# GpSimd's instructions in program order, the first expert's W2 squares in a chain of their own, and two experts' W1 products in halves of the tokens

## The chip, the cores and the metric

The kernel runs on one core of a Trainium2 chip. The metric is the device time of one execution in microseconds (us), the median of several runs. Five engines run their own instruction streams and wait for each other by semaphores: TensorE (PE in the profile), VectorE (DVE), ScalarE (ACT), GpSimd (POOL) and SyncE (SP, which only issues transfers here). Transfers are also issued by GpSimd, where rows are gathered or scattered by a list of row numbers.

## The reference, cut to what matters

First an attention over 8 batches and 8 heads of 576 positions (half of the heads with a band of 32 positions, half with every 32nd position), and then a layer of 8 experts on its output. The change is in the second part:

```python
def _moe_ref(x, w_gate, w1, w2):              # x: 4608 x 512, from the attention
    N, D = x.shape
    E = w_gate.shape[1]                        # 8
    cap = N // E                               # 576
    logits = x @ w_gate
    flat = logits.flatten()
    order = np.argsort(-flat)
    assigned = -np.ones(N, dtype=np.int64)
    counts = np.zeros(E, dtype=np.int64)
    for idx in order:
        tok, e = (int(idx) // E, int(idx) % E)
        if assigned[tok] >= 0 or counts[e] >= cap:
            continue
        assigned[tok] = e
        counts[e] += 1
        if (assigned >= 0).all():
            break
    out = np.zeros((N, D), dtype=np.float32)
    for e in range(E):
        mask = assigned == e
        h = np.maximum(x[mask] @ w1[e], 0.0)   # 576 x 1024
        out[mask] = h @ w2[e]                  # 576 x 512
    return out.astype(np.float32)
```

Each expert takes exactly 576 tokens, and which ones it takes depends on the experts that were filled before it.

## The kernel before, in words

Until about 262 us of the profiled execution the core does the attention, writes its rows to a scratch tensor in DRAM (`x_scr`) and finds the first expert's tokens. From then on it works through the experts, in the order in which they fill up, as phases 0 to 7; "expert 1" below is the expert of phase 1. A phase has these steps.

- **Search.** Some rounds narrow down the threshold at which the expert is full: VectorE compares (`cm`, L848), TensorE sums (L867, L876, L886), VectorE takes the next step (L871, L874, L884).
- **Indices.** The tokens above the threshold are numbered (L912 to L949), one-hot tiles are made (`ohl`, L992), 36 small TensorE products (L1001) and two more (L1012) turn them into a list of 576 row numbers, `idx` (L1016, L1017). Search and indices of a later expert run between the products of an earlier one.
- **Tokens.** `tokens()` has GpSimd gather the rows in five blocks of 128, 128, 128, 128 and 64 tokens (`xg`, L1168, from `x_scr`), and SyncE's queue transpose each block into `xt` (L1171). Blocks 0 to 2 of expert 0 are transposed by TensorE (L1154).
- **Weights.** W1 and W2 come in four loads of 512 KB each (`w`, L1041, SyncE's queue). ScalarE sums their squares (`jk`, L1045), from which a power of two is derived as a scale (L1051, L1056, L207). Then ScalarE makes the high halves (`w1h`, `w2h`, L1062) and VectorE the low ones (`w1l`, `w2l`, L1066), in float16, eight pieces of each matrix.
- **W1 products.** `hidden()` makes one of eight tiles of 128 hidden units for a list of column ranges (12 products a range, L1260); ScalarE takes the high half of the result (`hh`, L1266), VectorE the low half (`hl`, L1270). Expert 0 goes through all eight tiles for tokens 0 to 255 and then through all eight for tokens 256 to 575. The others do both 288-token halves of a tile before the next tile.
- **W2 products.** In `ffn()` token blocks 0 and 1 go first, as a pair (48 products, L1324), then the 64 tokens of block 4 as the tail (24 half-width products, L1312), then blocks 2 and 3 (24 products each, L1324). Within the pair the pieces of W2 are used in order, with the products `w2h·hh`, `w2l·hh`, `w2h·hl` for each block. ScalarE writes the result `y` (L1337; the tail's by ScalarE and VectorE, L1332 and L1333), and GpSimd scatters its rows to the output (L1338): five scatters per expert, which touch different rows.

The order of all this on TensorE, ScalarE, VectorE and SyncE is the order in which the program emits it (`manual_schedule`, with the engine sets `MAN` and `MAN1`, L49). GpSimd's order before is made by the compiler's own scheduler. The program's order comes from a planner that runs at build time: each side task (search of the next expert, fetch, splits, the low half of a tile) is a Python generator in the list `chains` with a due time. The loop at the end walks through the TensorE products, adds their assumed cost to `clock`, and advances every chain whose due time has come. `busy` holds the assumed end of what is queued on ScalarE and VectorE, `book()` adds to it, and `idle()` waits until it is short. The numbers `T_...` are due times in ns: `fetch()` of an expert yields `T_LOAD`, the time it allows from the request of the tokens until the expert may start, `T_W20` is the due time of expert 0's W2 squares, and the clock runs at double cost until `T_COLD`. The due times only set an order. Nothing on the chip waits for a clock.

All scatters write the same DRAM tensor, so that by the framework's rule a later one would wait for an earlier one. The kernel before takes this off by name:

```python
            for s in scat:
                tc.declare_no_dep(st.ins, s.ins, reason="rows of other tokens")
            scat.append(st)
```

## Time and profile before

| what | value |
|---|---|
| runs shown | 704.23, 706.38, 708.78 us (median 706.38) |
| profiled execution | 700.24 us, of which its span is 698.4 us |
| TensorE busy | 607.0 us (87%) |
| VectorE, ScalarE, GpSimd busy | 460.5, 320.0, 152.9 us |
| TensorE busy, 386 to 690 us | 299.78 of 304.00 us |
| TensorE busy, 296 to 304, 319 to 330, 376 to 386 us | 5.28 of 8.00, 6.17 of 11.00, 7.82 of 10.00 us |

The page of the profile gives busy times by engine, the same in 40 slices with the clock that TensorE was granted (PEclk), and the costliest groups of instructions with what ended the idle time before them. Other views answer for a stretch of time: what TensorE waited for, the single instructions in order, and the transfers with the time from issue to landing. Busy times of TensorE overlap from one instruction to the next, so that the distance between starts is what a product costs.

### The profile page before, as it was taken

The numbers are of one execution on the slowest core, as the hardware profiler recorded it, in microseconds if no ns is written. First come the engines' busy times: TensorE is split into PE (matmuls) and PEld (weight loads), VectorE is DVE, ScalarE is ACT, GpSimd is POOL, SyncE is SP. The second block draws the span as 40 slices with busy tenths as digits, with TensorE's granted clock in tenths as the row PEclk, the third lists the DMA queues.
The fourth block names the chain that finished last, engine by engine and source line by source line (L and its number), as shares of the span: only waits on it lengthen the run. The fifth ranks groups of instructions, "written<-read, shape, count | busy, mean of one in ns | idle before, by whom it ended". The sixth has DMA issues, their size and how long they took to land.

```text
span 698.4 us, 19162 instructions
## 1 busy us (share of the span) xinstructions
PE 607.0 (87%) x8044; PEld 400.2 (57%) x8044; DVE 460.5 (66%) x1371; ACT 320.0 (46%) x499; POOL 152.9 (22%) x151
## 2 busy tenths in 40 slices
PE   6768689887886449987998999999999999999993
PEld 3556466665665428544853864764764765755741
DVE  4588476776887778854886788886786864561200
ACT  3455336345443046433565465645545576572210
POOL 2044133233143020032032032023202122202011
PEclk9587767888899569998999999999999999999997
DMA  9989999899765064239167275368366296731010
GB/s 248 267 210 235 235 255 219 217 263 236 182 141 130 2 218 115 70 116 260 45 175 211 67 197 183 137 106 253 120 105 207 107 217 233 205 44 69 1 39 30
DMA packets 107081, 111.23 MB, mean 159 GB/s; under 512 B 75852, under 2 KB 83622, under 8 KB 106483
## 3 DMA queue, kind: packets, MB, share of 16 engines
q1 hardware_dynamic: 98915, 88.46, 49.4%
q0 software_dynamic: 7360, 21.15, 9.8%
q8 instruction: 63, 1.03, 0.6%
q10 hardware_dynamic: 720, 0.39, 0.2%
q14 instruction: 23, 0.19, 0.1%
HBM read 73.60 MB, written 18.87 MB: 132 GB/s over the span
## 4 chain that ended last, share of the span: by engine, by line
PE 36%; issue 17%; DVE 3%; POOL 2%; DMA 1%; SPq 0%; ACT 0%; POOLq 0%; ACTq 0%
PE ph L1260 17%; PE ph L1324 14%; PE ph L1312 2%; POOL out_dram L1338 1%; POOL xg L1168 1%; DMA w<-in_w_dram 1%; DMA xg<-x_scr,idx 1%; DVE w2l L1066 0%; SPq L1171 0%; PE ph L1154 0%; DVE hl L1270 0%; DVE ohl L992 0%; ACT w1h L1062 0%; PE ph L1201 0%; PE pr__8414 L1001 0%
## 5 line engine op out<-in xcount | busy, mean ns | idle before, releaser
L1260 PE MATMUL ph<-xt,w1h 128*128 128x288 f16 (+2 forms) x1024 | 174.7, 287 | 5.4 <-DMA xt<-xg 4.8
L1260 PEld LDWEIGHTS <-w1h 128*128 128x128 f16 x1024 | 97.5, 98 | 31.3 <-issue 3.7
L1260 PE MATMUL ph<-xt,w1l 128*128 128x288 f16 (+2 forms) x512 | 110.8, 287 | 0.0
L1324 PE MATMUL ph<-w2l,hh 128*128 128x512 f16 x256 | 98.3, 384 | 4.8 <-DVE w2l L1066 4.7
L1324 PE MATMUL ph<-w2h,hl 128*128 128x512 f16 x256 | 98.4, 384 | 0.0
L1324 PE MATMUL ph<-w2h,hh 128*128 128x512 f16 x256 | 97.9, 383 | 0.0
L1338 POOL DMA_INDIRECT out_dram<-y,idx x40 | 42.6, 1066 | 235.9 <-ACT y L1337 222.0
L1266 ACT ACTIVATE hh<-ph 128x576 f16<-128x576 f32 (+2 forms) x72 | 42.9, 596 | 99.7 <-PE ph L1260 94.3
L1045 ACT ACTIVATE jk<-w 128x1024 f16<-128x1024 f32 x64 | 67.3, 1052 | 41.5 <-DMA w<-in_w_dram 40.6
L1324 PEld LDWEIGHTS <-hh 128*128 128x128 f16 x512 | 48.6, 98 | 59.3 <-issue 8.6
L1168 POOL DMA_INDIRECT xg<-x_scr,idx x40 | 41.1, 1028 | 145.4 <-DVE idx L1016 65.0
L1270 DVE SCALAR_TENSOR_TENSOR hl<-ph,hh 128x576 f16<-128x576 f32 (+2 forms) x72 | 49.2, 684 | 30.7 <-ACT hh L1266 30.5
L379 ACT ACTIVATE pr<-spa 128x576 f32<-128x576 f32 x32 | 20.8, 650 | 97.5 <-PE spa L375 97.5
L1260 PEld LDWEIGHTS <-w1l 128*128 128x128 f16 x512 | 49.6, 98 | 12.6 <-issue 0.4
L1337 ACT ACTIVATE y<-ph,so 128x512 f32<-128x512 f32 x32 | 21.1, 684 | 75.2 <-PE ph L1324 73.3
L427 POOL TENSOR_TENSOR xos<-xs,xos 118x768 f16<-118x768 f32 x16 | 27.4, 1712 | 121.9 <-ACT xos L426 121.9
L396 PE MATMUL po<-v_s,pr 64*54 64x65 f32 (+1 forms) x768 | 42.8, 264 | 10.7 <-issue 6.4
L1066 DVE SCALAR_TENSOR_TENSOR w2l<-w,w_sw,w2h 128x512 f16<-128x512 f32 x64 | 46.2, 744 | 4.2 <-ACT w2h L1062 4.2
L1066 DVE SCALAR_TENSOR_TENSOR w1l<-w,w_sw,w1h 128x512 f16<-128x512 f32 x64 | 46.4, 744 | 3.8 <-ACT w1h L1062 3.7
L1062 ACT ACTIVATE w2h<-w,w_sw 128x512 f16<-128x512 f32 x64 | 42.7, 712 | 12.2 <-DVE w_sw L207 12.2
L1062 ACT ACTIVATE w1h<-w,w_sw 128x512 f16<-128x512 f32 x64 | 42.2, 712 | 9.5 <-DVE w_sw L207 8.2
L1324 PEld LDWEIGHTS <-hl 128*128 128x128 f16 x256 | 25.1, 98 | 32.8 <-issue 7.5
(616 smaller groups left out, 952.4 us busy)
## 6 DMA issues: line engine op xcount, KB each, us to landing
w<-in_w_dram SPq DMA_DIRECT2D x64, 512.0 KB
kl<-in_kl_dram SPq DMA_DIRECT2D x8, 608.0 KB
v_s<-in_ns_dram SPq DMA_DIRECT2D x16, 292.5 KB
v_l<-in_nl_dram SPq DMA_DIRECT2D x16, 292.5 KB
ql<-in_qt_dram SPq DMA_DIRECT2D x8, 576.0 KB
x_scr<-xol SPq DMA_DIRECT2D x8, 512.0 KB
ks<-in_ks_dram SPq DMA_DIRECT2D x7, 576.0 KB
qs<-in_qt_dram SPq DMA_DIRECT2D x7, 576.0 KB
```

The lines of the kernel that those rows point to most:

```text
L396: nc.tensor.matmul(po[r:r + n, j - j0], pr[k, o:o + n], u.vn[k, t, 2 * p + h], start=(j == j0), stop=(j == j1 - 1), skip_group_check=True)
L427: eng.tensor_tensor(u.xo[:nr, :, 1, c], xf, u.xo[:nr, :, 0, c], op=OP.subtract)
L1045: nc.scalar.activation(jk, wf[:, c * n4:(c + 1) * n4].rearrange("p c f -> p (c f)"), AF.Square, scale=1.41422, accum_out=sq[:, c:c + 1])
L1062: nc.scalar.activation(hi[:, c, f], wf[:, c, f], AF.Copy, scale=s_)
L1066: nc.vector.scalar_tensor_tensor(lo[:, c, f], wf[:, c, f], s_, hi[:, c, f], op0=OP.mult, op1=OP.subtract)
L1168: nc.gpsimd.indirect_dma_start(out=xg[:n], out_offset=None, in_=x_rows, in_offset=bass.IndirectOffsetOnAxis(ap=idx[:n, t:t + 1], axis=0))
L1260: nc.tensor.matmul(tile_[:, j, :w], wt[:, d, f * 128:(f + 1) * 128], xt[:, d // 2, xx, d % 2, c], start=(k == 0), stop=(k == 3 * DC - 1))
L1266: nc.scalar.activation(hv, src, AF.Relu)
L1270: nc.vector.scalar_tensor_tensor(lv, src, 0.0, hv, op0=OP.max, op1=OP.subtract)
L1324: nc.tensor.matmul(pair[:, u], a[:, f, (t + u) * 128:(t + u) * 128 + 128], w[:, f], start=(f == 0 and a is hh and w is w2h), stop=(f == FC ...
L1337: nc.scalar.activation(y, py, AF.Copy, scale=so[:, t:t + 1])
L1338: st = nc.gpsimd.indirect_dma_start(out=out_rows, out_offset=bass.IndirectOffsetOnAxis(ap=idx[:n, t:t + 1], axis=0), in_=y[:n], in_offset= ...
```

## The change

Five things are altered. GpSimd joins the engines whose instructions stand in program order. The squares and the scale of expert 0's W2 (`sums()`) become a chain that the planner may advance by itself; the chain that splits W1 and W2 still runs through it, and each of the four squares has a due time of its own instead of one for all. The first two experts (`HALVES`) make their W1 products in two ranges, tokens 0 to 255 and 256 to 575, in this order: tiles 0 to 3 for the first range, tiles 4 to 7 for both, tiles 0 to 3 for the second; their `fetch()` yields 8500 instead of 12000. `T_COLD` becomes 1500. And the list `scat` with its `declare_no_dep` is gone.

```diff
-MAN, MAN1 = {mybir.EngineType.PE}, {mybir.EngineType.Activation, mybir.EngineType.DVE, mybir.EngineType.SP}
+MAN, MAN1 = {mybir.EngineType.PE}, {mybir.EngineType.Activation, mybir.EngineType.DVE, mybir.EngineType.SP,
+                                       mybir.EngineType.Pool}
...
-T_LOAD, T_LOAD0, T_W20, T_LAND1, T_LAND2, T_TURN, T_COLD, CUT0, T_ROUND0 = 12000, 1500, 9000, 9000, 8500, 11000, 5000, 1, 1600
+HALVES, T_HALF, T_LOAD, T_LOAD0, T_W20, T_LAND1, T_LAND2, T_TURN, T_COLD, CUT0, T_ROUND0 = 2, 8500, 12000, 1500, (5000, 9500, 11500, 13000), 9000, 8500, 11000, 1500, 1, 1600
...
             def squares(land):
-                yield due(land)
                 for c in range(4):
+                    yield due(land if isinstance(land, int) else land[c])
                     yield from idle("s", 0)
                     square(c)
...
+            def sums():
+                yield from squares2(T_W20)
+                yield from scale2()
+
+            sums_ = sums()
+
             def later():
                 yield from splits1(CUT0)
-                yield from squares2(T_W20)
-                yield from scale2()
+                yield from sums_
                 yield from splits2()
...
                 chains.append([clock, bulk[-1]])
+                chains.append([clock, sums_])
...
-        yield T_LOAD
+        yield T_HALF if ph < HALVES else T_LOAD
...
-        if ph == 0:
+        if ph < HALVES:
             t0 = H0 // 128
-            for f in first[TURN_E:t0]:
-                f()
-            for c in (slice(0, H0), slice(H0, CAP)):
-                for f in range(FC):
-                    yield from hidden(ph, wts, xt, hh, hl, f, (c,), ps_h.tile([128, 2, 512], F32, name="ph"))
-                    if c.start == 0 and max(t0, TURN_E) <= t0 + f < len(first):
-                        first[t0 + f]()
+            part = slice(0, H0), slice(H0, CAP)
+            for u, f in [(0, f) for f in range(FC // 2)] + [(u, f) for f in range(FC // 2, FC) for u in range(2)] + \
+                    [(1, f) for f in range(FC // 2)]:
+                yield from hidden(ph, wts, xt, hh, hl, f, (part[u],), ps_h.tile([128, 2, 512], F32, name="ph"))
+                if ph == 0 and u == 0 and max(t0, TURN_E) <= t0 + f < len(first):
+                    first[t0 + f]()
...
-                        for c in (0, H0 if ph == 0 else 0):
+                        for c in (0, H0 if ph < HALVES else 0):
...
-                st = nc.gpsimd.indirect_dma_start(out=out_rows,
-                                                  out_offset=bass.IndirectOffsetOnAxis(ap=idx[:n, t:t + 1], axis=0),
-                                                  in_=y[:n], in_offset=None)
-            for s in scat:
-                tc.declare_no_dep(st.ins, s.ins, reason="rows of other tokens")
-            scat.append(st)
+                nc.gpsimd.indirect_dma_start(out=out_rows,
+                                             out_offset=bass.IndirectOffsetOnAxis(ap=idx[:n, t:t + 1], axis=0),
+                                             in_=y[:n], in_offset=None)
```

In the changed kernel L1168 becomes L1175, L1338 becomes L1344, L1066 becomes L1067, L1012 becomes L1013, L1312 becomes L1318 and L1324 becomes L1330.

On GpSimd, from the first scatter of expert 0 on, the kernel before has these instructions. `out_dram<-y,idx` is a scatter, `xg<-x_scr,idx` a gather, `DMASW` with a number is the landing of an earlier transfer that GpSimd issued, `Activation` and `DVE` are the engines that write `y` or `idx`, `DMAHW` is the landing of a transfer of SyncE's queue.

```order
L1338 DMA out_dram<-y,idx 4608x512 [waits Activation_49] x2
L1168 DMA xg<-x_scr,idx 128x1024 [waits DMASW7_49,DVE_49]
L1168 DMA xg<-x_scr,idx 128x1024 [waits DMASW0_49,PE_49]
L1168 DMA xg<-x_scr,idx 128x1024 [waits DMAHW5_49,DMASW2_49]
L1168 DMA xg<-x_scr,idx 128x1024 [waits DMAHW6_49,DMASW3_49,DMASW1_49]
L1168 DMA xg<-x_scr,idx 64x1024 [waits PE_49]
L1338 DMA out_dram<-y,idx 4608x512 [waits DVE_49]
L1338 DMA out_dram<-y,idx 4608x512 [waits DMASW4_49,Activation_49]
L1338 DMA out_dram<-y,idx 4608x512 [waits DMASW5_49,Activation_49]
L1168 DMA xg<-x_scr,idx 128x1024 [waits DMAHW6_49,DMASW6_49,DVE_49]
```

The changed kernel has at the same place:

```order
L1344 DMA out_dram<-y,idx 4608x512 [waits Activation_49]
L1344 DMA out_dram<-y,idx 4608x512 [waits DMASW4_49,Activation_49]
L1344 DMA out_dram<-y,idx 4608x512 [waits DMASW5_49,DVE_49]
L1175 DMA xg<-x_scr,idx 128x1024 [waits DMASW7_49,DVE_49]
L1175 DMA xg<-x_scr,idx 128x1024 [waits DMASW0_49,PE_49]
L1175 DMA xg<-x_scr,idx 64x1024 [waits PE_49]
L1344 DMA out_dram<-y,idx 4608x512 [waits DMASW6_49,Activation_49]
L1344 DMA out_dram<-y,idx 4608x512 [waits DMASW4_49,Activation_49]
L1344 DMA out_dram<-y,idx 4608x512 [waits DMASW5_49,Activation_49]
L1344 DMA out_dram<-y,idx 4608x512 [waits DMASW7_49,DMASW6_49,Activation_49]
L1175 DMA xg<-x_scr,idx 128x1024 [waits DMAHW6_49,DMASW0_49,DVE_49]
```

(Two of expert 1's five gathers are left out of this piece.) Two scatters of expert 0 stood ahead of expert 1's gathers, and now three do. The gathers of expert 2 stood ahead of all scatters of expert 1, and now stand behind the first two of them. Each scatter but the first now waits for the landing of the scatter ahead of it: the `DMASW4` of the second is the landing of the first, the `DMASW5` of the third that of the second, and so on. In the kernel before, the `DMASW` of a scatter is a transfer eight issues back.

On VectorE, at the end of expert 0's W2 splits, with expert 1's indices between them, the kernel before has (`sc`, `slot`, `ohh`, `rv` and `ohl` belong to the indices; rows left out stand between these):

```order
L1066 SCALAR_TENSOR_TENSOR w2l<-w_4037,w_sw_4039,w2h 128x512
L943 TENSOR_SCALAR off<-sc 128x72
L949 TENSOR_TENSOR slot<-off 128x36
L1066 SCALAR_TENSOR_TENSOR w2l<-w_4037,w_sw_4039,w2h 128x512
L974 CAST si<-slot 128x36
L984 TENSOR_TENSOR rv_3688<-ohh,val 128x972
L992 TENSOR_TENSOR ohl_4772<-sh,iota 128x768
L961 TENSOR_TENSOR L<-L,pe_4751 128x288
L1066 SCALAR_TENSOR_TENSOR w2l<-w_4037,w_sw_4039,w2h 128x512 x3
```

And the changed kernel:

```order
L932 TENSOR_TENSOR sc<-sc 128x36
L1067 SCALAR_TENSOR_TENSOR w2l<-w_4037,w_sw_4039,w2h 128x512 x2
L944 TENSOR_SCALAR off<-sc 128x72
L950 TENSOR_TENSOR slot<-off 128x36
L975 CAST si<-slot 128x36
L985 TENSOR_TENSOR rv_3688<-ohh,val 128x972
L993 TENSOR_TENSOR ohl_4789<-sh,iota 128x768
L1067 SCALAR_TENSOR_TENSOR w2l<-w_4037,w_sw_4039,w2h 128x512
L962 TENSOR_TENSOR L<-L,pe_4770 128x288
```

Three of the eight low halves stood behind the indices, and now one does, the eighth.

On TensorE, the last two index products of expert 1 (`pick`, L1012) stood between the tail products of expert 0:

```order
L1312 MATMUL ph<-w2h,hh 64x512
L1012 LDWEIGHTS p_4843
L1012 MATMUL pr__4868<-pick,p_4843 64x10
L1312 LDWEIGHTS hh
L1312 MATMUL ph<-w2l,hh 64x512
```

In the changed kernel they stand behind all 24 of them:

```order
L1318 MATMUL ph<-w2h,hl 64x512
L1330 LDWEIGHTS hh
L1330 MATMUL ph<-w2h,hh 128x512
L1013 LDWEIGHTS p_4871
L1013 MATMUL pr__4891<-pick,p_4871 64x10
L1330 LDWEIGHTS hh
```

They moved by 17 products: 16 of the tail and one of block 2. The 36 products L1001 that feed them moved from inside the pair into the tail.

More of the change, by code (lines that the diff above doesn't have):

```diff
@@ L743, in band_stride_attention_then_capacity_moe @@
     x_rows = x_scr.rearrange("n a d -> n (a d)")
-    scat, closed, first = [], [], []
+    closed, first = [], []
     ready, emitted = set(), set()
```

## The prediction

> **What bounds the kernel now.** I read the page first: which engine is busy, and when.
>
> ```profile
> span 698.4 us, 19162 instructions
> PE 607.0 (87%) x8044; PEld 400.2 (57%) x8044; DVE 460.5 (66%) x1371; ACT 320.0 (46%) x499; POOL 152.9 (22%) x151
> PE   6768689887886449987998999999999999999993
> ```
>
> TensorE carries the span. The experts begin at the 16th slice (17.5 us each), and from the 21st on its digit is 9. The change touches nothing ahead of the experts, so the question is which microseconds TensorE loses behind 262 us. Its busy time by stretches, and what it waited for from 255 us on, say where they lie:
>
> ```profile
> 296.00:304.00 8.00, 5.28 (x40) 2.29 (x42) 4.36 (x9) 0.96 (x2) 0.00 (x0) 0.79 0.37 149
> 319.00:330.00 11.00, 6.17 (x37) 3.75 (x35) 3.15 (x10) 0.69 (x1) 1.00 (x1) 0.69 1.06 282
> 376.00:386.00 10.00, 7.82 (x53) 4.04 (x52) 4.72 (x14) 3.98 (x7) 1.88 (x2) 0.83 0.29 110
> 386.00:690.00 304.00, 299.78 (x2325) 188.48 (x2323) 185.22 (x546) 151.46 (x250) 57.30 (x56) 1.00 0.47 133
> ...
> PE ph L1260 <- DMA xt<-xg: 4.8, 2, 2.9
> PE ph L1324 <- DVE w2l L1066: 4.7, 5, 2.8
> ...
> PE pr__5819 L876 <- DVE r L874: 2.2, 1, 2.2
> ```
>
> (The first number behind the stretch is TensorE's busy time; the last three are its granted clock, the DMA share and GB/s.) From 386 us on it is 99% busy at clock 1.00. The losses lie in three places: A (296 to 304, W2's low halves of expert 0), B (319 to 330, expert 1's tokens) and C (376 to 386, a search step). The single instructions give their prices:
>
> ```profile
> 298.72 0.58 PE L1324 MATMUL ph<-w2l,hh 128*128 128x512 f16 x1 [2.80 <-DVE w2l L1066]
> 302.07 0.38 PE L1324 MATMUL ph<-w2h,hh 128*128 128x512 f16 x1
> 302.28 0.38 PE L1324 MATMUL ph<-w2l,hh 128*128 128x512 f16 x1
> ...
> 305.44 1.05 PE L1312 MATMUL ph<-w2h,hh 128*64 128x512 f16 x8
> ...
> 319.76 0.17 PE L886 MATMUL pr__5037<-ih,ones_j 128*128 128x1 f16 x1
> 322.84 0.40 PE L1260 MATMUL ph<-xt,w1h 128*128 128x288 f16 x1 [2.91 <-DMA xt<-xg]
> 325.16 0.90 PE L1260 MATMUL ph<-xt,w1h 128*128 128x288 f16 x3 [1.92 <-DMA xt<-xg]
> 328.80 0.64 PE L1260 MATMUL ph<-xt,w1h 128*128 128x288 f16 x2
> ...
> 365.36 1.05 PE L1312 MATMUL ph<-w2h,hh 128*64 128x512 f16 x8
> ...
> 380.49 0.17 PE L876 MATMUL pr__5819<-r,fold 68*128 68x8 f16 x1 [2.19 <-DVE r L874]
> 383.90 0.69 PE L1260 MATMUL ph<-xt,w1h 128*128 128x288 f16 x4
> ```
>
> At full clock a W2 product costs 302.28 - 302.07 = 0.21 us. In A the 8 products from 298.72 to 302.07 took 3.35 instead of 1.7 us, so that a wait of 2.80 us brought 1.6 us of half speed after it: A = 4.4. In B the waits are 2.91 and 1.92, the one product between them cost 0.3 too much, and from 325.16 to 328.80 some 1.75 of 3.64 us are half speed: B = 6.9. In C, 2.19 plus about 1.6: C = 3.8. Two later waits for `w2l` in expert 1 make 0.7. Together 15.8 us are lost here, and everything that the change moves lies here.
>
> [...] In A, after 2.80 us of idleness, products ran at half speed. [...]
>
> **The change, part by part.** *Scatters that wait for each other.* The removed `declare_no_dep` and the order rows say that each scatter now waits on GpSimd for the previous one's landing, with the gathers queued behind it. GpSimd in the trace:
>
> ```profile
> 306.52 1.03 POOL L1338 DMA_INDIRECT out_dram<-y,idx  x1 [46.52 <-ACT y L1337]
> 307.85 0.98 POOL L1338 DMA_INDIRECT out_dram<-y,idx  x1 [0.30 <-ACT jk L1045]
> 309.14 1.15 POOL L1168 DMA_INDIRECT xg<-x_scr,idx  x1 [0.30 <-DVE cm L848]
> ...
> 356.87 0.99 POOL L1168 DMA_INDIRECT xg<-x_scr,idx  x1 [34.95 <-DVE idx L1016]
> ...
> 367.48 1.04 POOL L1338 DMA_INDIRECT out_dram<-y,idx  x1 [3.22 <-ACT y L1337]
> 368.83 1.21 POOL L1338 DMA_INDIRECT out_dram<-y,idx  x1 [0.30 <-issue]
> ...
> 682.95 0.98 POOL L1338 DMA_INDIRECT out_dram<-y,idx  x1 [3.65 <-ACT y L1337]
> 688.12 0.97 POOL L1338 DMA_INDIRECT out_dram<-y,idx  x1 [4.20 <-ACT y L1337]
> ```
>
> and the landings, from issue, of the two scatters issued at 306.52 and 307.85, of the one at 367.48, of the one at 370.76 (under weight loads), and of all ten in 296 to 395 us:
>
> ```profile
> out_dram<-y,idx POOLq DMA_INDIRECT x2, 2.8
> ...
> out_dram<-y,idx POOLq DMA_INDIRECT x1, 3.0
> ...
> out_dram<-y,idx POOLq DMA_INDIRECT x1, 6.5
> ...
> out_dram<-y,idx POOLq DMA_INDIRECT x10, 3.4
> ```
>
> So one wait costs 2.8 to 6.5 us where 1.3 us of issue stood; I take 2.8 next to expert 0 and 3.0 next to expert 1. Let P be the start of the tail (305.44, 365.36). Expert 0: scatters at P + 1.1, P + 4.0 and P + 6.9, first gather 1.3 later at X = P + 8.2; it was P + 3.7. Expert 1: first scatter P + 2.1, second P + 5.1, gathers of expert 2 at X = P + 6.4 (5.2 at the least, 9.9 with a landing of 6.5); they were 8.5 us ahead of P.
>
> [...]
>
> *Halves (B).* From X, expert 1's third block was in place at 322.84 (X + 13.7) and the fifth at 325.16 (X + 16.0). Both halves were needed at once; the first range now needs two blocks. One block less is 1.15 us by these two, so X + 12.5. A block's issue is 1.2 to 3.2 us long:
>
> ```profile
> L1171 SPq DMA_TRANSPOSE xt<-xg x37: 1192/1452/3178, 261.5 to 613.8; - x37
> ```
>
> which bounds it to X + 10.5. So products start at P + 20.7 (18.7 at the least). TensorE gets there at P + 15.3: 319.93 - 305.44 = 14.5, plus the 36 products L1001 that now stand behind the pair,
>
> ```profile
> 303.24 1.30 PE L1001 MATMUL pr__4806<-ohl,rv 128*32 128x64 f16 x36
> ```
>
> 1.2, less 0.4 of search that moves on. Stall 5.4 and 1.75 of half speed: 7.15 against 6.9, **+0.3** (-1.8 to +3). What the halves save, the two waits eat. The remaining blocks land while tiles 0 to 3 of the first range run (48 products, 5.2 us).
>
> *Expert 2's tokens (C).* The five blocks are needed at once, at X + 16.0: P + 22.4. TensorE's work from P to there is 383.90 - 365.36 less C's 3.8 = 14.7 us. Stall 7.7 and 1.7 of half speed make 9.4; C's own wait falls into it. 9.4 - 3.8 = **+5.6**. SyncE's queue now has expert 2's W2 loads ahead of these transposes, which speaks for no less; with faster transposes (X + 14) and the shortest landing it is +2, with a landing of 6.5 it is +9.5.
>
> *The W2 squares (A).* Seven low halves move ahead, but the eighth stays behind the indices on VectorE:
>
> ```profile
> 290.10 0.17 DVE L749 TENSOR_REDUCE mm<-pr__4646 128x1 f32<-128x8 f32 x1 [0.38 <-PE pr__4646 L886]
> ...
> 291.99 0.74 DVE L1066 SCALAR_TENSOR_TENSOR w2l<-w,w_sw,w2h 128x512 f16<-128x512 f32 x1
> 292.65 0.19 DVE L943 TENSOR_SCALAR off<-sc 128x72 f32<-128x72 f16 x1
> ...
> 296.15 1.49 DVE L992 TENSOR_TENSOR ohl<-sh,iota 128x768 f16<-128x768 f16 x3
> 297.56 0.45 DVE L961 TENSOR_TENSOR L<-L,pe 128x288 f32<-128x288 f32 x1
> ```
>
> From L886's product, some 0.2 us ahead of 290.10: 0.2 + 1.9 to `sc`, two low halves at 0.66, then from 292.65 to 297.56 4.9 less the 0.66 of the low half between them, and the eighth at 0.74: 8.4 us. TensorE has 24 W2 products and two small ones between, 5.3 us. Stall 3.1 and 1.6: 4.7 against 4.4, **+0.3** (-4.4 if VectorE were early enough, +1).
>
> *The rest.* In halves the PSUM tiles of expert 0 and 1 turn over twice as often, with `hh` queued behind the W2 squares: **+0.3** (0 to 1.3). Expert 1's eight low halves of W2 share VectorE with 16 instead of 8 `hl`: **+0.5** (0 to 1). `T_COLD` and `T_HALF` only set the order above. The last two scatters are 5.2 us apart, more than the median landing of 3.4, and from expert 3 on the gathers stand well ahead of their need, with no wait in 386 to 690 us: **0**, by that cover.
>
> Sum: +0.3 + 5.6 + 0.3 + 0.3 + 0.5 = +7.0; I take off 1.0 since the 16.0 was measured at a DMA share of 1.06 and expert 2's gathers need not meet that. **+6.0 us**. On the profiled execution (span 698.4, itself 700.24) that is 706.2; on the median of the runs, 6.1 above it, 706.38 + 6.0 = 712.4.
>
> **The rivals.** *Faster: waits vanish.* The eighth low half is ready in time (A gone, -4.4), and the halves make B shrink while the landings cost what an issue costs (X = P + 4.5; two blocks at P + 16.5, stall 1.2: -5.7), with C' as short as its bounds (+2): with the small terms -7.3, 699.1. For it: the seven early splits, and landings of only 2.8 us. Against: the eighth stands behind 8.4 us of VectorE work, and a landing is waited for in full. It decides if VectorE ends the indices 3 us sooner.
>
> *Slower: long landings.* The scatters next to expert 1's gathers landed in 6.5 us under the weight loads. If such landings fall on the waits of expert 0 (one of two, +3.5) and of expert 1 (+3.5), it is +13, 719.4. For it: DMA shares over 1 at 319 to 330 us, and W2 loads that now stand ahead of expert 2's transposes. Against: next to P the landings were 2.8 to 3.0. It decides from one landing over 4 us.
>
> *No effect.* The gathers are late anyway and the other parts give back what C' takes: 0, 706.4. For it: A, B and C all end in other waits already. Against: expert 2's gathers started 8.5 us ahead of P and can't now.
>
> **How the numbers follow.** Forecast +6 (own range +1 to +10): 0.55. Long landings: 0.20. No effect: 0.12. Faster: 0.13. The range 699 to 720 takes in the two outer cases' centres and leaves their far halves out, under 2 in 10. A change of 1%, 7.1 us, is about what can be told from none. The forecast's range crosses +7: a little over a third of it lies above. Slower by over 1%: 0.20 + 0.20 = 0.40; faster: half of its case and a little for what I don't see, 0.12; within: 0.48.
>
> **What would show it.** Right: on GpSimd the second scatter of expert 0 starts about 2.9 us after the first, and expert 2's first gather after P of expert 1, with TensorE's longest wait (7 to 8 us) before expert 2's first W1 product; a wait of about 3 us for the eighth `w2l`; expert 1's first W1 product near P + 20. Wrong: expert 2's products start without a wait, the `w2l` wait is gone, or TensorE waits somewhere behind 400 us.

## The result, and the profile after

The changed kernel takes 712.30 us (median of 20 runs, 703.51 to 716.63), the kernel before 705.86 us (20 runs, 701.28 to 710.01). The ratio is 1.008, with a 95% interval of 1.0054 to 1.0106: 0.8% slower, some 5.6 us. Ratios, here and below, leave out executions more than 1.5% above the fastest of their kernel, where the two medians (6.4 us apart) take in all 20, and the one profiled execution that is so slow, that of the kernel with T_COLD at 5000, is not compared.

The page of the changed kernel, and what its TensorE waited for from 290 us on (us in total, times, longest):

```profile
span 710.1 us, 19178 instructions
PE 612.9 (86%) x8044; PEld 405.4 (57%) x8044; DVE 463.0 (65%) x1379; ACT 320.5 (45%) x507; POOL 153.6 (22%) x151
...
PE ph L1267 <- DMA xt<-xg: 12.3, 3, 5.2
PE ph L1330 <- DVE w2l L1067: 4.4, 3, 2.9
PE pr__6069 L868 <- DVE cm L849: 0.5, 1, 0.5
```

A, B and C are the three places of loss that the prediction names. The waits for tokens went from 4.8 to 12.3 us. The waits for W2's low halves hardly moved (4.7 to 4.4), and C's wait for a search step, 2.2 us before, is 0.2. The two spans are 11.7 us apart, more than the medians. Of this, 4.1 us lie ahead of expert 0's first W1 product (at 261.71 us before and 265.77 after), where the order of the instructions is the same in both but for one `w1h` on ScalarE in the last 2 us. From that product to the last W2 product it was 425.0 us and is 432.0: 7.0 us more, of which 0.9 lie in expert 0's W1 products (26.6 and 27.6 us). The last 0.6 us lie behind the last W2 product. TensorE's instructions where most of the 7.0 us come from:

```profile
306.30 0.58 PE L1330 MATMUL ph<-w2l,hh 128*128 128x512 f16 x1 [2.87 <-DVE w2l L1067]
308.52 1.35 PE L1318 MATMUL ph<-w2h,hh 128*64 128x512 f16 x8
...
328.55 0.38 PE L1267 MATMUL ph<-xt,w1h 128*128 128x256 f16 x2 [3.83 <-DMA xt<-xg]
...
368.54 0.41 PE L1318 MATMUL ph<-w2h,hh 128*64 128x512 f16 x2
...
388.89 0.40 PE L1267 MATMUL ph<-xt,w1h 128*128 128x288 f16 x1 [5.20 <-DMA xt<-xg]
392.57 0.90 PE L1267 MATMUL ph<-xt,w1h 128*128 128x288 f16 x3 [3.28 <-DMA xt<-xg]
```

A's wait stands nearly unchanged (2.87 us, 2.80 before). Expert 1 starts at P + 20.0, where it ran from P + 19.7 before (P is the start of the tail, 308.52 and 368.54 here). Expert 2 runs from P + 24.0 instead of P + 18.5: here the time went. GpSimd shows why:

```profile
309.61 1.03 POOL L1344 DMA_INDIRECT out_dram<-y,idx  x1 [46.03 <-ACT y L1343]
313.20 0.98 POOL L1344 DMA_INDIRECT out_dram<-y,idx  x1 [2.56 <-DMA out_dram<-y,idx]
316.69 1.05 POOL L1344 DMA_INDIRECT out_dram<-y,idx  x1 [2.51 <-DVE rmn L968]
318.04 0.99 POOL L1175 DMA_INDIRECT xg<-x_scr,idx  x1 [0.30 <-issue]
...
372.11 0.97 POOL L1344 DMA_INDIRECT out_dram<-y,idx  x1 [40.12 <-ACT y L1343]
375.59 0.97 POOL L1344 DMA_INDIRECT out_dram<-y,idx  x1 [2.51 <-issue]
376.87 1.35 POOL L1175 DMA_INDIRECT xg<-x_scr,idx  x1 [0.30 <-DVE r L875]
```

The landing that the second and the third scatter wait for comes 2.7 to 2.8 us after the issue of the one ahead, so that scatters now start 3.5 to 3.6 us apart where it was 1.3. (The name in the brackets is what ended last by the profile. For the third scatter it is a VectorE instruction of the indices, but its own `y`, which VectorE wrote from 313.71 on for 0.74 us, had long been there.) Expert 1's first gather stands at P + 9.5 (P + 3.7 before), expert 2's at P + 8.3 (8.5 us ahead of P before). Behind this, from 396 to 700 us, TensorE is busy for 300.88 of 304.00 us, as before.

### The profile page after: what moved, and what is told of

It reads as the page before. It is cut to its first block, busy times and chain, and to the rows that moved or that the text cites. A ratio compares the mean times of both kernels' runs of the same rounds, so it can differ in the third digit from the quotient of the medians.

```text
span 710.1 us, 19178 instructions
## 1 busy us (share of the span) xinstructions
PE 612.9 (86%) x8044; PEld 405.4 (57%) x8044; DVE 463.0 (65%) x1379; ACT 320.5 (45%) x507; POOL 153.6 (22%) x151
## 5 line engine op out<-in xcount | busy, mean ns | idle before, releaser
L1267 PE MATMUL ph<-xt,w1h 128*128 128x288 f16 (+2 forms) x1024 | 180.3, 289 | 14.1 <-DMA xt<-xg 12.3
L1267 PE MATMUL ph<-xt,w1l 128*128 128x288 f16 (+2 forms) x512 | 117.1, 289 | 0.0
L1344 POOL DMA_INDIRECT out_dram<-y,idx x40 | 42.4, 1061 | 300.4 <-ACT y L1343 189.9
L1330 PE MATMUL ph<-w2l,hh 128*128 128x512 f16 x256 | 97.4, 380 | 4.5 <-DVE w2l L1067 4.4
L1330 PE MATMUL ph<-w2h,hl 128*128 128x512 f16 x256 | 97.4, 381 | 0.0
L1330 PE MATMUL ph<-w2h,hh 128*128 128x512 f16 x256 | 97.2, 380 | 0.0
L1330 PEld LDWEIGHTS <-hh 128*128 128x128 f16 x512 | 47.8, 98 | 54.6 <-issue 4.2
L1175 POOL DMA_INDIRECT xg<-x_scr,idx x40 | 41.1, 1028 | 88.3 <-DVE idx L1017 39.1
L1067 DVE SCALAR_TENSOR_TENSOR w2l<-w,w_sw,w2h 128x512 f16<-128x512 f32 x64 | 46.5, 743 | 4.2 <-ACT w2h L1063 4.2
L1063 ACT ACTIVATE w1h<-w,w_sw 128x512 f16<-128x512 f32 x64 | 42.4, 713 | 12.3 <-DVE w_sw L208 10.9
L1067 DVE SCALAR_TENSOR_TENSOR w1l<-w,w_sw,w1h 128x512 f16<-128x512 f32 x64 | 46.6, 744 | 2.0 <-ACT w1h L1063 1.8
L1330 PEld LDWEIGHTS <-hl 128*128 128x128 f16 x256 | 25.0, 98 | 33.2 <-issue 6.2
```

Of the source, the lines that this page charges most:

```text
L1063: nc.scalar.activation(hi[:, c, f], wf[:, c, f], AF.Copy, scale=s_)
L1067: nc.vector.scalar_tensor_tensor(lo[:, c, f], wf[:, c, f], s_, hi[:, c, f], op0=OP.mult, op1=OP.subtract)
L1175: nc.gpsimd.indirect_dma_start(out=xg[:n], out_offset=None, in_=x_rows, in_offset=bass.IndirectOffsetOnAxis(ap=idx[:n, t:t + 1], axis=0))
L1267: nc.tensor.matmul(tile_[:, j, :w], wt[:, d, f * 128:(f + 1) * 128], xt[:, d // 2, xx, d % 2, c], start=(k == 0), stop=(k == 3 * DC - 1))
L1330: nc.tensor.matmul(pair[:, u], a[:, f, (t + u) * 128:(t + u) * 128 + 128], w[:, f], start=(f == 0 and a is hh and w is w2h), stop=(f == FC ...
L1344: nc.gpsimd.indirect_dma_start(out=out_rows, out_offset=bass.IndirectOffsetOnAxis(ap=idx[:n, t:t + 1], axis=0), in_=y[:n], in_offset=None)
```

## The experiments

Each ratio is that to the kernel before, with its 95% interval. The last column is the time in the profiled execution from expert 0's first W2 product to the last W2 product of all. It leaves out the attention and the first W1 products, whose clock differed between executions (the last section). It is one execution each, in which a stretch of half speed, worth 1.7 us, can fall or not (the last section too).

| kernel | ratio | first to last W2 product, us |
|---|---|---|
| before | 1 | 398.4 |
| changed | 1.0080 (1.0054 to 1.0106) | 404.5 |
| changed, no waits between scatters | 1.0019 (0.9970 to 1.0069) | 399.3 |
| changed, gathers first | 1.0113 (1.0072 to 1.0155) | 404.5 |
| changed, GpSimd by the scheduler | 1.0012 (0.9972 to 1.0052) | 400.0 |
| before, waits between scatters | 0.9967 (0.9928 to 1.0007) | 398.3 |
| changed, T_COLD 5000 | 0.9992 (0.9947 to 1.0037) | not compared |
| the same, six buffers for y | 0.9951 (0.9917 to 0.9986) | 395.1 |
| changed, gathers first, six buffers for y | 0.9964 (0.9928 to 1.0000) | 395.9 |
| changed, T_COLD 3000 | 0.9929 (0.9889 to 0.9970) | 392.2 |
| changed, no chain for W2's squares | 0.9977 (0.9936 to 1.0017) | 396.6 |
| T_COLD 3000, halves for expert 0 alone | 1.0037 (0.9997 to 1.0076) | 396.8 |
| T_COLD 3000, no waits between scatters | 0.9897 (0.9839 to 0.9954) | 389.6 |
| the same, expert 2's squares later | 0.9954 (0.9912 to 0.9995) | 392.1 |

### The waits, with everything else in place

The waits are taken off by name again, and a small memset stands between the scatters, so that two of them are never neighbours in GpSimd's order.

```diff
+    spacer = rt.tile([128, 1], F32, name="spacer", bufs=1)
...
+                nc.gpsimd.memset(spacer, 0.0)
-                nc.gpsimd.indirect_dma_start(out=out_rows,
+                st = nc.gpsimd.indirect_dma_start(out=out_rows,
...
+            for s in scat:
+                tc.declare_no_dep(st.ins, s.ins, reason="rows of other tokens")
+            scat.append(st)
```

> The changed kernel, with a one-column memset on GpSimd ahead of each scatter and the declare_no_dep back, so that GpSimd keeps its program order but no scatter waits for the landing of another. All instructions of the other engines stand as in the changed kernel. Theory S (the waits for landings hold up the gathers): the second scatter of expert 0 starts 1.3 to 1.6 us after the first (3.6 in the changed kernel), expert 1's first gather at P + 6.5 (P + 9.5), expert 2's at P + 6.3 (P + 8.3); TensorE's wait for expert 1's tokens falls from 3.8 to about 1, the two for expert 2's from 8.5 to about 6.5; 4 to 6 us faster than the changed kernel, so about level with the kernel before (within 2.5 us). Theory O (the place of the gathers in the program holds them up, the waits come on top of nothing): 0 to 1.5 us faster than the changed kernel, still 5 us over the kernel before.

Theory S held in the main: the ratio falls from 1.008 to 1.002, some 4.3 us (the two intervals overlap by a little). GpSimd in this kernel, and TensorE's waits for tokens:

```profile
311.00 1.03 POOL L1346 DMA_INDIRECT out_dram<-y,idx  x1 [47.45 <-ACT y L1344]
312.34 0.98 POOL L1346 DMA_INDIRECT out_dram<-y,idx  x1 [0.18 <-ACT jk L1047]
316.37 0.91 POOL L1346 DMA_INDIRECT out_dram<-y,idx  x1 [2.93 <-DVE ohn L194]
317.58 0.99 POOL L1176 DMA_INDIRECT xg<-x_scr,idx  x1 [0.30 <-DVE pen L968]
...
PE ph L1268 <- DMA xt<-xg: 9.5, 3, 4.1
```

The second scatter follows after 1.3 us, but the third still waits 2.9 us, now for its own `y` (the tail's result, which VectorE writes from 315.35 on for 0.74 us; the name in the brackets is an instruction of the indices that ended after it), and the gathers wait with it: P + 7.7 instead of the P + 6.5 that I expected, and 3.25 instead of 1 us of waiting. So the waits for landings cost most of the loss, 4.3 of the 5.6 us by the ratios and 5.2 of 6.1 by the traces; of the 5.2, 1.7 is half speed that the wait for expert 1's tokens brought in the changed kernel and not here. The place behind a scatter that isn't ready delays the gathers by itself. What that costs in time can't be told from nothing (1.0019).

### The waits alone, and the change without its part on GpSimd

The kernel before, without its three lines on `scat`, and GpSimd's order left to the scheduler:

> The kernel before with the declare_no_dep taken out and nothing else: scatters wait for each other's landings, GpSimd's order is the scheduler's, which now puts three gathers of expert 1 between the first and the second scatter of expert 0. TensorE's, VectorE's and ScalarE's orders are those of the kernel before. Theory S in its narrow form (a wait costs only if gathers are queued behind it): expert 1's first gather at P + 2.5, its last within 1 us of the kernel before, expert 2's gathers ahead of all scatters of expert 1 as before; within 1.5 us of the kernel before. Rival W (each wait costs wherever it stands): 4 us or more slower.

The narrow form held. 0.9967 can't be told from no change, and the stretch is 398.3 us against 398.4. The scheduler put three gathers between the first and the second scatter. When the second one's turn comes the first has landed, so that it starts at once, and so do the two gathers behind it:

```profile
306.09 1.02 POOL L1338 DMA_INDIRECT out_dram<-y,idx  x1 [47.76 <-ACT y L1337]
307.42 0.98 POOL L1168 DMA_INDIRECT xg<-x_scr,idx  x1 [0.30 <-issue]
...
311.37 0.99 POOL L1338 DMA_INDIRECT out_dram<-y,idx  x1 [0.30 <-issue]
312.67 0.97 POOL L1168 DMA_INDIRECT xg<-x_scr,idx  x1 [0.30 <-issue]
```

Expert 2's gathers stand ahead of all scatters of expert 1 here, and these scatters do wait (they start at P + 2.1, P + 7.0 and P + 14.7), with no gather behind them. So the missing lines alone cost nothing where the scheduler is free to move the gathers. The other way round, the changed kernel with `Pool` out of `MAN1` and the `declare_no_dep` back:

> The changed kernel without its part on GpSimd: GpSimd's order is left to the scheduler and the declare_no_dep is back. What is left is the W2 squares' chain, the halves and the due times. The scheduler puts expert 2's third to fifth gather behind two scatters of expert 1. Theory S: expert 1's first gather at P + 6.5, expert 2's first at P + 1.5 and its last at about P + 9 (P + 13.7 in the changed kernel), 5 to 8 us faster than the changed kernel, and within 2 us of the kernel before. Theory P (the new order of the other engines is at fault, the waits are not): it stays 4 us or more above the kernel before.

1.0012: within 2 us of the kernel before, and 4.8 us faster than the changed kernel, a little less than the 5 to 8 that S said. TensorE still waits 2.55 us for expert 1's tokens and 4.48 us for expert 2's last blocks: here two scatters stand between expert 2's second and third gather, and its indices come at P + 2.3, 11 us later than before.

### The gathers ahead of the scatters

Scatters are kept back until the next expert's gathers have been emitted.

```diff
+                if ph + 1 < E and ph + 1 not in asked:
+                    late.append(scatter)
+                else:
+                    scatter()
...
         asked[ph] = clock
+        while late:
+            late.pop(0)()
```

> The changed kernel, where the scatters of an expert are emitted behind the gathers of the next expert if these have not been emitted yet; each scatter still waits for the landing of the one ahead. Theory S: expert 1's first gather at P + 5, as soon as its indices are there (P + 9.5 in the changed kernel), expert 2's at P + 1.5 (P + 8.3); TensorE's waits for tokens fall from 3.8 to 0 or 1 and from 8.5 to about 2; 9 to 13 us faster than the changed kernel, 3 to 6 us faster than the kernel before. Theory D (transfers are slow under the weight loads whenever they start): the gathers start earlier but the blocks land hardly earlier, and the gain is under 4 us.

A miss: 1.0113, no better than the changed kernel. The waits for tokens did go, and others came. TensorE's waits, and ScalarE:

```profile
PE pr__5011 L887 <- DVE g L885: 6.3, 1, 6.3
PE pr__5812 L877 <- DVE r L875: 5.3, 1, 5.3
...
330.28 0.69 ACT L1345 ACTIVATE y<-ph,so 128x512 f32<-128x512 f32 x1 [8.38 <-DMA out_dram<-y,idx]
```

`y` has three buffers. Expert 0's first scatter starts behind five gathers, and with them and the transposes under way it lands only after 7.2 us. Until then ScalarE can't write the fourth `y`, the high halves of W1 wait behind that on ScalarE, VectorE behind them, and TensorE for VectorE's search step. To test this, the same with `name="y", bufs=6`:

> The run with the gathers first (changed kernel, gathers of the next expert emitted ahead of the scatters, waits between scatters kept) with six buffers for y. Theory Y: the two waits of 6.3 and 5.3 us for VectorE (a search step) are gone, expert 1's first gather stays at P + 6.5 since its indices are late, expert 2's at P + 2.5; 5 to 9 us faster than the changed kernel. If VectorE was late for another reason: as the run with three buffers, 7 us over the kernel before.

1.0113 falls to 0.9964, some 10 us, and the two waits for a search step are gone. TensorE's longest waits are now:

```profile
PE ph L1332 <- DVE w2l L1067: 4.4, 3, 2.9
PE ph L1269 <- DMA xt<-xg: 3.8, 2, 2.1
PE ph L1269 <- ACT y L1345: 1.5, 1, 1.5
```

The first is A and its like. The 3.8 us for tokens are two waits, expert 1's and expert 2's; expert 1's indices come late (first gather at P + 6.5), as expected.

### One number, T_COLD

> The changed kernel with one number put back: T_COLD is 5000 again. Everything else stays, the waits between scatters too. The planner then emits expert 1's index products at the start of the tail (P + 0.1 of TensorE work, P + 4 in the changed kernel) and expert 2's 7.6 us of work ahead of P (0.3 behind it), so that both sets of gathers stand ahead of the scatters. Theory K (T_COLD moved the indices, and that put the gathers behind the scatters): expert 1's first gather at P + 1.5, expert 2's 6 us and more ahead of P, no wait for their tokens above 1 us. Theory Y (the three buffers of y fill up when a scatter stands behind the gathers, as in the run with the gathers first, where ScalarE waited for a buffer): TensorE waits 4 to 6 us for a search step between expert 0's last W2 products. K alone: 10 to 13 us faster than the changed kernel, 4 to 6 faster than the kernel before. K and Y: 4 to 8 us faster than the changed kernel. Rival S alone (only the waits matter, and they are all still there): no faster than the changed kernel.

0.9992: 6 us faster than the changed kernel, level with the kernel before, with all the waits between scatters kept. By the time it is K and Y together. With six buffers:

> The run before it with six buffers for y instead of three. Theory Y: the wait for a search step in expert 0's last W2 products is gone; 9 to 13 us faster than the changed kernel, 3 to 6 us faster than the kernel before. If y is not it: as the run before it, within 1.5 us.

0.9951, 2.9 us less than with three buffers, and 3.5 us under the kernel before. K shows in the trace: expert 1's first gather stands at P + 0.6, expert 2's 7.6 us ahead of P, and TensorE waits for no tokens. But another large wait remains, and it is not for `y`. TensorE, VectorE and ScalarE in this kernel:

```profile
376.60 0.16 PE L887 MATMUL pr__5735<-ih,ones_j 128*128 128x1 f16 x1 [5.48 <-DVE g L885]
...
375.73 0.74 DVE L1339 SCALAR_TENSOR_TENSOR y<-ph,so,yl 64x512 f32<-64x512 f32 x1 [6.77 <-ACT yl L1338]
...
373.84 1.06 ACT L1046 ACTIVATE jk<-w 128x1024 f16<-128x1024 f32 x1 [6.34 <-DMA w<-in_w_dram]
```

ScalarE stands 6.3 us at a square of expert 2's W2, whose load has not landed; `yl`, VectorE and TensorE are behind it. That is also what C was in the kernel before, where ScalarE's square waited 3.25 us and VectorE 2.66 for `w1h`:

```profile
374.32 1.06 ACT L1045 ACTIVATE jk<-w 128x1024 f16<-128x1024 f32 x1 [3.25 <-DMA w<-in_w_dram]
...
379.35 0.75 DVE L1066 SCALAR_TENSOR_TENSOR w1l<-w,w_sw,w1h 128x512 f16<-128x512 f32 x1 [2.66 <-ACT w1h L1062]
```

In the changed kernel C's wait is gone: SyncE issues all eight loads of expert 2's weights between 352.5 and 368.6 us there, ahead of its transposes (from 380.7), where the last four stood behind the transposes before (369.4 and 360.8).

With T_COLD at 3000 the order has two scatters ahead of expert 1's gathers, and all eight low halves ahead of expert 1's one-hot tiles:

> The changed kernel with T_COLD at 3000, the waits between scatters kept. By the order all eight low halves of expert 0's W2 then stand ahead of the one-hot tiles of expert 1 on VectorE, two scatters stand ahead of expert 1's gathers (three in the changed kernel), and expert 2's gathers ahead of expert 1's scatters. Theory: the wait of 2.9 us for the low half (A, with its half speed 4.4 us) is gone or under 1; expert 1's first gather at P + 6, products from P + 16.5, wait about 1; no wait above 3 us for expert 2's tokens; 11 to 15 us faster than the changed kernel, 5 to 8 us faster than the kernel before. Rival (VectorE works the same amount and TensorE waits for something else in the same place): A turns into a wait of 2 to 3 us for the one-hot tiles, and the gain over the kernel before is under 3 us.

0.9929, some 5 us faster than the kernel before, and A is gone. TensorE's waits from 290 us on:

```profile
PE pr__5850 L868 <- DVE cm L849: 5.1, 1, 5.1
PE ph L1330 <- DVE w2l L1067: 1.9, 2, 1.6
PE ph L1267 <- DMA xt<-xg: 1.1, 1, 1.1
```

The wait of 5.1 is that of the late square again, which the expectation did not have. ScalarE:

```profile
373.95 1.06 ACT L1046 ACTIVATE jk<-w 128x1024 f16<-128x1024 f32 x1 [6.10 <-DMA w<-in_w_dram]
```

### The chain of the squares, and the halves

The changed kernel without `chains.append([clock, sums_])`, with T_W20 at 9000:

> The changed kernel with the chain of the W2 squares undone (the squares only within the chain of the splits, due at 9000). TensorE's order is that of the changed kernel; on VectorE six instead of seven low halves of expert 0's W2 stand ahead of expert 1's indices, two behind. If the chain gains nothing while the last low half stays behind the indices: TensorE's wait there stays 2.5 to 3.5 us and the time stays within 1.5 us of the changed kernel. If the chain gains as such: a longer wait, by 1.5 us and more.

A miss, and in one point the expectation was wrong by itself: TensorE's order is not that of the changed kernel, since the planner moved the index products too. The wait for the last low half is 2.9 us, as expected, so the chain by itself gains nothing at A. But the kernel is 7 us faster than the changed one (0.9977): two scatters instead of three stand ahead of expert 1's gathers.

```profile
302.95 1.02 POOL L1343 DMA_INDIRECT out_dram<-y,idx  x1 [44.57 <-ACT y L1342]
306.54 1.07 POOL L1343 DMA_INDIRECT out_dram<-y,idx  x1 [2.56 <-DMA out_dram<-y,idx]
307.91 1.01 POOL L1174 DMA_INDIRECT xg<-x_scr,idx  x1 [0.30 <-DVE pen L967]
```

The first gather is at P + 6.0, and expert 1 starts at P + 15.9 with no wait, 4.2 us earlier than in the changed kernel; expert 2 runs from P + 21.6, 2.4 us earlier. Then the halves, undone for expert 1 in the kernel with T_COLD at 3000 (`HALVES = 1`, by which expert 1's `fetch()` yields 12000 again):

> The kernel with T_COLD at 3000, and the halves undone for expert 1 (HALVES = 1), so that its first W1 product needs three token blocks and the rest five. Scatters, gathers and indices of experts 0 to 2 stand as with the halves. If the halves are worth what the blocks' landings say: first gather at P + 6.6, five blocks in place at P + 22, TensorE there at P + 15.7; 5 to 8 us slower than with the halves. If the wait only moves to tiles 4 to 7: within 2 us.

1.0037 against 0.9929: 7.6 us slower by the times, 4.6 by the traces. The halves for expert 1 are worth about that when the gathers are early: the waits for tokens rise from 1.1 to 3.8 us, and expert 1 runs from P + 20.5 instead of P + 17.5.

### Towards a faster version

The kernel with T_COLD at 3000 and the memset and `declare_no_dep` of the first experiment:

> The kernel with T_COLD at 3000, and the scatters freed of their waits (a one-column memset between them and the declare_no_dep back). Two scatters stand ahead of expert 1's gathers in either. Theory K (with the indices early the waits between scatters hardly matter): expert 1's first gather 2 to 2.5 us earlier, its wait of 1.1 gone, 1 to 3 us faster than with the waits. Theory S (each wait is worth its landing): 6 us and more faster.

0.9897, 1.0% faster than the kernel before and the fastest here by its ratio. It is 2.3 us less than with the waits, as K said, though the two intervals overlap; the traces differ by 2.6 us. No wait for tokens is left:

```profile
PE pr__5860 L869 <- DVE cm L850: 4.7, 1, 4.7
PE ph L1331 <- DVE w2l L1068: 1.9, 2, 1.6
PE pr__6937 L869 <- DVE cm L850: 0.5, 1, 0.5
```

To take the 4.7 away too, expert 2's W2 squares were made due later:

```diff
-            sent[ph] = max(...) + T_LAND2
+            sent[ph] = max(...) + (16000 if ph == 2 else T_LAND2)
```

> The run before it, and expert 2's W2 squares due 7.5 us later, so that on ScalarE none of them stands between the last y of expert 1 and the high halves of expert 2's W1. Theory Q (the wait of 5 us for a search step in expert 1's W2 products is ScalarE held at a square whose weights are still on their way, with VectorE and TensorE behind it): that wait falls under 1, 4 to 6 us faster than the run before it, 8 to 12 us faster than the kernel before. Rival: the wait moves to expert 2's start, for its tokens, which land at about the same time, and the gain is under 2 us.

The wait is gone, and expert 2 starts 5.8 us earlier (111.1 instead of 116.9 us after expert 0's first product), but it is given back: 0.9954. The waits are now one of 2.1 us for expert 2's low halves of W2, whose scale comes later, and this in expert 2's W2 products:

```profile
435.29 0.69 ACT L1344 ACTIVATE y<-ph,so 128x512 f32<-128x512 f32 x1 [8.27 <-DMA out_dram<-y,idx]
...
437.76 0.17 PE L878 MATMUL pr__6660<-r,fold 68*128 68x8 f16 x1 [3.82 <-DVE r L876]
```

The three buffers of `y` again: expert 3's five gathers now stand right ahead of expert 2's first scatter, which starts at 426.04 us, and ScalarE waits for a buffer until 435.29. Six buffers in this version were not tried.

## Why the prediction was right, and where not

**The time.** Forecast 712.4, measured 712.3; forecast +6.0, measured about 5.6 by the ratio, 6.4 by the medians and 7.0 in the two traces. The mechanism is the one that the forecast named: gathers behind scatters that wait for landings. Without the waits some 4 of the 5.6 us go. That the sum came out so close is in part luck: its largest errors, in B and C below, nearly cancel. "Long landings" didn't occur next to P: there the scatters landed in 2.7 to 2.8 us. "Waits vanish" and "no effect" are out, by the rows above.

**The terms.** In two terms the sizes were off, in opposite directions.

- *A wait* was priced at the landing, 2.8 to 3.0 us. From issue to issue it is 3.5 to 3.6: some 0.8 us pass between the landing and the next issue. Expert 1's first scatter came at P + 3.6 instead of P + 2.1 as well. So the gathers of expert 1 came at P + 9.5, not P + 8.2, and those of expert 2 at P + 8.3, not P + 6.4.
- *B* was +0.3. The two blocks landed 10.5 us after the first gather, the lower bound, not 12.5, and TensorE got there at P + 16.2, not P + 15.3. So expert 1 started at P + 20.0, close to the forecast's P + 20.7, since a later gather and a faster landing offset each other. The wait was 3.83 us instead of 5.4, and with 1.7 us of half speed B is 5.5 against 6.9: -1.4.
- *C* was +5.6. Five blocks took 15.7 us (16.0 taken), but from a later gather: waits of 5.20 and 3.28, one product between them and about 2.6 us of half speed make some 11.3 instead of 9.4, so +7.5. The one long wait of 7 to 8 us that was to show it came as these two. The 1.0 that I took off for quieter transfers was not there. (The upper end of this term is +9.1 by its own figures, 9.9 + 16.0 - 14.7 + 1.7 - 3.8, not +9.5.)
- *A* was +0.3: 2.87 us of waiting against 3.1 forecast, and against 2.80 before. That the low halves behind the indices decide is shown from both sides: with all eight early the wait is gone, with two behind it is still 2.9.
- *The halves' small cost* was +0.3 within 0 to 1.3. TensorE waited 1.2 us for `hl` in expert 0, where it did not before. *Expert 1's low halves of W2* were +0.5. Its waits for them went from 0.7 to 1.1 us, +0.3, and expert 2's from 1.0 to 0.5.
- A small misreading bears on nothing: in the kernel before, the digit of the 22nd slice, where C lies, is 8 and not 9.

**What the prediction priced in the wrong place.** It said that `T_COLD` and `T_HALF` "only set the order above" and charged all to the scatters. The price was right for the order as it stood, but the order was no property of GpSimd's part. One number at 3000 instead of 1500, with every wait kept, turns 1.008 into 0.993, and so does, for the most part, undoing the squares' chain. The waits and the place of the gathers are both needed for the loss: waits without gathers behind them cost nothing that can be told (0.9967), and gathers behind scatters without waits neither (1.0019).

**The clock.** The forecast charged half speed of 1.6 to 1.8 us to each of its three stalls. In the changed kernel that held in price: half speed followed the waits of 2.87 and 3.83 us, as it followed that of 2.80 before, and those of 5.20 and 3.28 brought 2.6 us of it. As a rule for every such wait it does not hold. In the kernel without the squares' chain the wait of 2.86 us at A brought none, and in that without waits between scatters the wait of 3.25 us for expert 1's tokens brought none. Both of these lie across an edge of the 3.41 us stretches of their execution, which leaves at most 1.65 us on either side (the last section), so that here the forecast was lucky too.

## What to carry to other kernels

A wait on GpSimd, which in these traces starts its transfers in the order of its queue, cost what stood behind it: some 4 of the 5.6 us with gathers there, nothing that can be told without (0.9967). Before a dependency comes back, look which instructions of other chains are queued behind the waiting one, and put those ahead of it. Then count the buffers that the delayed instruction holds. In the kernel with the gathers first the engine that refills them stopped next (ScalarE, for 8.38 us), and what was queued behind it with it (TensorE, for 6.3 us). Where a planner sets the order from assumed times, a number that costs nothing itself can move a gather past a scatter (T_COLD at 3000 instead of 1500 turned 1.008 into 0.993), so that parts of a change can't be priced one by one: read the order that comes out.

## What the runs showed of the hardware

- In the two traces of the kernel before and the changed one, half speed (a granted clock of 0.50) came in stretches of 3.41 us or multiples of it, and not from the edge of a wait. It lasted 3.41, 6.83 and 3.41 us in the kernel before (from 298.6, 322.5 and 380.5 us, at A, B and C) and 3.41, 3.41 and 10.24 us in the changed kernel (from 305.8, 329.6 and 387.7 us). All these edges of one execution lie whole multiples of 3.41 us apart. Four stretches with their clock (the third number from the end), the first two from the kernel before, the third from the changed kernel, the fourth from that without waits between scatters:

```profile
298.65:302.00 3.35, 3.28 (x8) 1.13 (x8) 1.71 (x4) 0.00 (x0) 0.00 (x0) 0.50 0.13 51
...
322.55:329.30 6.75, 4.54 (x26) 2.80 (x26) 0.27 (x2) 0.00 (x0) 0.00 (x0) 0.50 1.03 301
...
387.70:397.90 10.20, 5.73 (x32) 3.69 (x33) 1.89 (x6) 0.00 (x0) 1.97 (x2) 0.50 0.41 98
...
324.70:331.50 6.80, 3.56 (x33) 2.34 (x30) 3.20 (x9) 0.94 (x2) 1.69 (x4) 1.00 1.15 241
```

  If the two traces are cut into stretches of 3.41 us at these edges, and TensorE's waits of over 0.1 us in each stretch at full clock are added up, from expert 0's first W1 product to the last W2 product, six stretches have more than 1.51 us: 2.70, 2.58 and 2.19 us in the kernel before (ending at 298.6, 322.5 and 380.5 us), 2.32, 2.32 and 3.41 us in the changed kernel (ending at 305.8, 329.6 and 387.7 us). Half clock followed each of the six. It followed none of the others, the largest of which has 1.51 us. What waits between 1.51 and 2.19 us bring, these two traces don't show. So the wait of 2.19 us at C, which lies in one stretch, was followed by half speed. The wait of 3.25 us in the last line was not: in that kernel the products behind A's wait went from half to full speed at about 311.1 us, and counted from there in steps of 3.41 us, an edge at about 328.1 us cuts this wait into 1.65 and 1.6. In the kernel without the squares' chain they went from half to full speed at about 383.4 us; counted back from there, an edge at about 298.1 us cuts A's wait of 2.86 us into 1.5 and 1.35. In the changed kernel the wait of 3.83 us is cut into 1.5 and 2.3, and products ran at full speed from 328.55 to 329.5 us and then at half speed until 332.9, a loss of 1.7 us.
- Expert 0's W1 products, which stand in the same order in the changed kernel and in that with GpSimd left to the scheduler, took 27.6 and 29.9 us. The granted clock in their first 8 to 9 us (the third number from the end) was 1.00 in the one and 0.71 in the other:

```profile
265.70:274.00 8.30, 7.41 (x85) 6.45 (x85) 6.86 (x20) 6.33 (x13) 0.00 (x0) 1.00 0.95 209
...
258.90:268.00 9.10, 8.94 (x76) 7.26 (x75) 5.42 (x15) 4.93 (x11) 0.00 (x0) 0.71 0.75 167
```

  A comparison of two profiled executions has to start behind such a stretch, or it takes clock, 2.3 us here, for an effect. (The kernel before had full clock there as well, so that the 0.9 us between its W1 products and those of the changed kernel are not of this kind.)
- A scatter of 128 rows landed in 2.7 to 2.8 us in the changed kernel where the DMA engines were busy for a share of 0.24 meanwhile (those issued at 309.61, 313.20 and 375.59 us). Issued right behind five gathers with their transposes under way, it took 4.4 us (T_COLD at 3000) to 7.3 us (gathers first, six buffers for `y`), and 5.5 us in the changed kernel, at a share of 1.17.
